# Five of six groups of an MLP's second product by Strassen's seven block products

## The chip, the core and the metric

The kernel runs on one core of a Trainium2 chip. The metric is the device time of one execution in microseconds (us), the median of several runs. The engines are named as in the profile: PE (TensorE, matrix products), DVE (VectorE), ACT (ScalarE), POOL (GpSimd) and SP (SyncE, which issues most DMAs). PE reads its operands from SBUF and writes to PSUM; DVE and ACT read both memories, POOL reads SBUF here.

## The reference

Linear attention with decay, then an MLP with a snake activation, on one set of 3072 tokens (4 batches of 768) with 512 features (8 heads of 64):

```python
for b in range(nb):                       # attention, block by block
    intra = einsum(qb, kb) * Dmask; intra = einsum(intra, vb)
    inter = einsum(qb * lam_pow, kv_state)
    out[:, :, sl] = intra + inter
    kv_state = lam_block * kv_state + einsum(kb_dec, vb)
x = out as (3072, 512)
h = x @ w_in                              # (3072, 512) @ (512, 2048)
s = sin(alpha * h)
g = h + s * s / (alpha + 1e-09)
return g @ w_out                          # (3072, 2048) @ (2048, 512)
```

Inputs and output are float32; the kernel multiplies in bf16 and accumulates in float32.

## The kernel before

The tokens are cut into six groups of 512 (`g` 0 to 5). A group has four attention units (`u` 0 to 23: one batch, four heads, 256 positions) and an MLP on its 512 tokens.

**A unit.** SP loads q, k and v (`ld`, 256 KB each). They are cast to bf16 (`cq`, `ck`, L717/L719), v is scaled (`sv`, L725 on POOL), q and k are transposed (`tq`, `tk` on PE with copies `e0`, `e1`; from unit 9 on by DMA). On PE follow scores (L759), products with the state (L869), the output (L882) and the update of the state (L793), from unit 8 on in one `step`. DVE masks the scores (`mm`, L767) and evicts the output into `xt` (`oe`, L901); ACT copies the state out (`kc`, L803); POOL decays and carries it (`d0`, `d1`, `n0`, `n1`: L818, L821, L859).

**The MLP.** A group has 16 f1 blocks, one for each 128 of the 2048 hidden columns: four matmuls of 128x128x512 into one PSUM bank (L916), a sine on ACT (`sn`, L923), a square on ACT or POOL (`sq`, L930/L932), and on DVE `g` = square times 1/alpha plus h into `gall` (L935), which releases the bank. The second product, f2, has for each of four token tiles (`m`) 16 matmuls of 128x128x512 (L952), in four blocks `f2_g_m_j`, added up in one bank; ACT copies it out (`ev`, L958) and SP stores it (`out`, L980). The last tile of group 5, `f2_5_3`, is made in two halves of 256 columns (`end0`, `end1`, `send0`, `send1`).

**Buffers.** f1 blocks, f2 tiles and some early transposes share four PSUM banks ("f"); of them f2 tiles may hold at most three at a time ("part"). `gall` has four buffers of a whole group.

**The order.** No loop gives the order. All steps are handed to a planner (`Plan`) as operations with a cost by engine, what they wait for, and a rank (`vt`); it plays them through and emits each engine's instructions in the order that it finds. `TUNE` shifts ranks and fixes engines, one entry per step. Each engine then works its instructions off in that order. On PE, f1 blocks of one group stand between steps of the units and f2 blocks of earlier groups; where f2 blocks are at hand they fill PE while the other engines work.

The costs that the planner uses for f1 and f2 blocks and the wait of f1 for a free `gall` buffer are these lines:

```python
mm = add(f"f1_{g}_{f}_{hb}", on("PE", .865 * x + (0.01 if hb is not None else 0)), ...)
op = add(f"f2_{g}_{m}_{j}", on("PE", .865), deps, vt, None, ...)
for g in range(NGB, NG):
    for f in range(NFC):
        f1_mm[g, f].after += [f2_last[g - NGB, m] for m in range(4)]
```

Of the kernel before, what the change touches and what calls it, by code (L numbers as in the profile page):

```python
# [167 lines left out]
def kernel(  # L168
# [11 lines left out]
    nc = tc.nc  # L180
# [15 lines left out]
        "lam": (0.0, 'ACT'), "iden": (0.0, 'POOL'), "lamb": (0.0, 'PE'), "tabc": (0.0, 'DVE'),  # L196
        "tab1": (1.2, 'POOL'), "tabm": (852.8, 'DVE'), "tabi": (-21.2, 'POOL'),
        "tabd": (-499.1, 'POOL'), "tab2": (-428.0, 'DVE'), "tab0": (-2.1, 'PE'),
        "tab4": (-818.2, 'DVE'), "tab3": (-962.3, 'ACT'), "alq": (0.0, 'ACT'),
# [1100 lines left out]
    for g in range(2, NG):  # L1300
        for f in range(NFC):
            make_f1(g, f, None)
# [45 lines left out]
```

## Time and profile before

| | |
|---|---|
| Time, median of 3 runs | 221.42 us (221.19 to 221.84) |
| Span of the profiled execution, first to last instruction | 218.2 us |
| The profiled execution's own time | not listed; the median lies 3.2 us above the span |
| Granted TensorE clock | 1.000 |
| PE busy | 211.9 us (97%), 2102 matmuls |
| DVE / ACT / POOL busy | 121.0 (55%) / 141.3 (65%) / 124.6 us (57%) |
| f1 matmuls (L916) | 388 |
| f2 matmuls (L952) | 400, of which 32 of 256 columns |
| HBM read / written | 27.27 / 6.29 MB |

Busy time of PE counts pipelined matmuls with modelled ends, so that what a matmul costs is better read from how many follow each other in a stretch than from the mean of one. On the other engines too an instruction may be recorded as starting a little before the last one's end. The chain of waits follows the end of the program back through whatever released each step. Idle time of an engine that is not the bottleneck costs nothing.

### The profile page before, as it was taken

The page shows a single profiled execution, that of the slowest core. Times are in us where ns is not written, and L with a number is a line of the kernel's source. Part 1 is how long each engine was busy: PE and PEld are TensorE (multiplying, and loading weights), DVE is VectorE, ACT ScalarE, POOL GpSimd, SP SyncE. Part 2 cuts the span into 40 slices and gives each one's busy share as a digit, 9 for nine tenths or more (in the row PEclk, how much of TensorE's full clock was granted, in tenths as well). Part 3 has the DMA queues.
Part 4 walks back from the last instruction along what each step waited for, and adds up shares of the span by engine and source line. Part 5 has one row for each costly group of instructions (what it writes and reads, how often), then busy time and mean ns, then how long its engine had stood idle before and what let it go on. Part 6 is the DMA issues. An engine that isn't in the chain of part 4 may idle for free.

```text
span 218.2 us, 5305 instructions
## 1 busy us (share of the span) xinstructions
PE 211.9 (97%) x2102; PEld 108.3 (50%) x2102; DVE 121.0 (55%) x176; ACT 141.3 (65%) x252; POOL 124.6 (57%) x209
## 2 busy tenths in 40 slices
PE   8999999999999999999999999999999999999994
PEld 3556644455544555545654545554444444444463
DVE  3457676457368974657794797975345451311100
ACT  3454699656499664878968787476778695634220
POOL 7959599768989899999898755611101100001000
PEclk9999999999999999999999999999999999999999
DMA  5999999898999999969999964020220221203164
GB/s 148 302 287 146 192 206 207 240 292 247 264 240 209 217 263 268 240 175 235 301 152 224 267 58 99 0 51 0 50 48 0 51 50 24 60 11 74 27 141 98
DMA packets 62139, 33.65 MB, mean 154 GB/s; under 512 B 17938, under 2 KB 59170, under 8 KB 62114
## 3 DMA queue, kind: packets, MB, share of 16 engines
q1 hardware_dynamic: 57776, 29.04, 59.5%
q0 software_dynamic: 4224, 4.19, 12.0%
q8 instruction: 16, 0.26, 0.5%
q10 hardware_dynamic: 114, 0.07, 0.1%
q14 instruction: 9, 0.07, 0.1%
HBM read 27.27 MB, written 6.29 MB: 154 GB/s over the span
## 4 chain that ended last, share of the span: by engine, by line
PE 90%; POOL 4%; issue 2%; ACT 1%; DVE 1%; POOLq 0%; ACTq 0%
PE hps L916 35%; PE ops L952 33%; PE bz L989 6%; PE sp L759 3%; PE okv L952 3%; PE okv L882 2%; PE pt L735 2%; PE okv L869 2%; PE okv L793 1%; POOL vb L725 1%; POOL kvs L859 1%; POOL qk L719 1%; PE kp L793 1%; DVE gall L935 1%; ACT s L923 1%
## 5 line engine op out<-in xcount | busy, mean ns | idle before, releaser
L935 DVE SCALAR_TENSOR_TENSOR gall<-s,r_sb,hps 128x512 bf16<-128x512 bf16 (+1 forms) x97 | 69.8, 740 | 63.7 <-ACT s L930 47.8
L916 PE MATMUL hps<-xt,w_in_sb 128*128 128x512 bf16 (+1 forms) x388 | 91.9, 377 | 1.4 <-DVE gall L935 0.8
L952 PE MATMUL ops<-w_out_sb,gall 128*128 128x512 bf16 (+1 forms) x368 | 83.1, 370 | 0.0
L923 ACT ACTIVATE s<-hps,alpha_sb 128x512 bf16<-128x512 f32 (+1 forms) x97 | 65.4, 679 | 25.9 <-PE hps L916 24.7
L952 PEld LDWEIGHTS <-gall 128*128 128x128 bf16 x400 | 38.5, 98 | 41.7
L916 PEld LDWEIGHTS <-w_in_sb 128*128 128x128 bf16 x388 | 36.5, 98 | 43.2 <-issue 2.6
L932 POOL TENSOR_TENSOR s<-s 128x512 bf16<-128x512 bf16 x21 | 21.9, 1041 | 51.9 <-ACT s L923 51.9
L930 ACT ACTIVATE s<-s 128x512 bf16<-128x512 bf16 (+1 forms) x76 | 46.6, 623 | 1.7
L767 DVE TENSOR_TENSOR sm<-sp,mask 128x1024 bf16<-128x1024 f32 x24 | 29.3, 1220 | 4.6 <-PE sp L759 4.5
L725 POOL TENSOR_TENSOR vb<-st_v,R 128x512 bf16<-128x512 f32 x24 | 25.0, 1045 | 2.5 <-DMA st_v<-in_v_dram 2.5
L958 ACT COPY ob<-ops 128x512 f32<-128x512 f32 x21 | 12.3, 584 | 20.2 <-PE ops L952 20.2
L821 POOL TENSOR_TENSOR kvbd<-kvx,LBD 128x256 bf16<-128x256 f32 x32 | 19.7, 614 | 2.5
L818 POOL TENSOR_TENSOR kvx<-kva,kvs 128x128 f32<-128x128 f32 x32 | 14.6, 456 | 7.8 <-ACT kva L803 7.7
L901 DVE TENSOR_TENSOR xt<-okv,ET 128x512 bf16<-128x512 f32 x24 | 16.5, 686 | 3.1 <-PE okv L882 2.8
L989 PE MATMUL bz<-const-bfloat16-1.0 128*128 128x256 bf16 (+1 forms) x69 | 16.4, 311 | 1.5 <-PEq L1332 0.8
L719 POOL CAST qk<-st_q 128x512 bf16<-128x512 f32 x19 | 11.5, 612 | 2.5 <-PE okv L793 2.5
L719 POOL CAST qk<-st_k 128x512 bf16<-128x512 f32 x17 | 10.4, 613 | 0.8 <-DMA st_k<-in_k_dram 0.8
L759 PE MATMUL sp<-qt 64*64 64x128 bf16 x384 | 10.0, 221 | 0.0
L882 PE MATMUL okv<-sm,vb 64*64 64x128 bf16 x384 | 9.7, 218 | 0.0
L859 POOL TENSOR_TENSOR kvs<-kvx,ET 128x128 f32<-128x128 f32 x24 | 9.4, 403 | 0.0
L803 ACT COPY kva<-okv 128x256 f32<-128x256 f32 (+1 forms) x16 | 5.0, 314 | 6.6 <-PE okv L793 6.4
L742 ACT COPY qt<-pt 128x512 bf16<-128x512 bf16 x9 | 5.2, 590 | 6.2 <-PE pt L735 6.2
(63 smaller groups left out, 110.7 us busy)
## 6 DMA issues: line engine op xcount, KB each, us to landing
st_q<-in_q_dram SPq DMA_DIRECT2D x24, 256.0 KB, 5.1
st_k<-in_k_dram SPq DMA_DIRECT2D x24, 256.0 KB, 5.3
st_v<-in_v_dram SPq DMA_DIRECT2D x24, 256.0 KB, 5.0
out_dram<-ob SPq DMA_DIRECT2D x46, 128.0 KB, 2.5
w_out_sb<-in_moe_w_out_dram POOLq DMA_DIRECT2D x4, 512.0 KB, 11.9
w_in_sb<-in_moe_w_in_dram POOLq DMA_DIRECT2D x2, 512.0 KB, 6.4
w_in_sb<-in_moe_w_in_dram POOLq DMA_DIRECT2D x1, 768.0 KB, 9.6
w_in_sb<-in_moe_w_in_dram POOLq DMA_DIRECT2D x1, 256.0 KB, 6.4
```

What stands on the lines that cost most here:

```text
L719: ENGINE[op.eng].tensor_copy(out=o, in_=i)
L725: ENGINE[op.eng].tensor_tensor(out=T[u, "vb"][:], in0=T[u, "v"][:].rearrange("p h two e -> p two h e"), in1=R[:, :, hs].unsqueeze(3).to_br ...
L759: nc.tensor.matmul(out=T[u, "sp"][half[c], hd, par, hp, :], lhsT=QT[half[hd], 1, par, hp, half[c]], rhs=QT[half[hd], 0, :, hp, half[c]], s ...
L767: V.tensor_tensor(out=T[u, "sm"][:].rearrange("p hd par hp i -> p (hd par) hp i"), in0=T[u, "sp"][:].rearrange("p hd par hp i -> p (hd par ...
L821: G.tensor_tensor(out=bd[:], in0=X.unsqueeze(2).to_broadcast([P, 2, 2, D]), in1=LBD[:, hs, :].unsqueeze(3).to_broadcast([P, 2, 2, D]), op= ...
L916: op.ins = nc.tensor.matmul(out=op.tile[:, cols], lhsT=w_in_sb[:, c, f * P:(f + 1) * P], rhs=xt[g][:, c].rearrange("p b c i -> p (b c i)") ...
L923: A.activation(out=op.tile[:, cols], in_=mm.tile[:, cols], func=ACTF.Sin, scale=alpha_sb[:, f:f + 1])
L930: A.activation(out=op.tile[:, cols], in_=s1, func=ACTF.Square)
L932: ENGINE[op.eng].tensor_tensor(out=op.tile[:, cols], in0=s1, in1=s1, op=ALU.mult)
L935: V.scalar_tensor_tensor(out=gall[g][:, f, cols], in0=sq.tile[:, cols], scalar=r_sb[:, f:f + 1], in1=mm.tile[:, cols], op0=ALU.mult, op1=A ...
L952: op.ins = nc.tensor.matmul(out=first.tile[:, cols], lhsT=gall[g][:, f, m * P:(m + 1) * P], rhs=w_out_sb[:, f, cols], start=(f == 0), stop ...
L989: nc.tensor.matmul(out=bz[:, :w], lhsT=nc.const_aps.tensor(1.0, [P, P], BF16), rhs=nc.const_aps.tensor(1.0, [P, w], BF16), start=True, sto ...
```

## The change

For groups 1 to 5 the second product is cut into 2x2 blocks: 256 tokens by the even or odd hidden tiles, and even or odd hidden tiles by 256 output columns. Instead of eight block products, seven are made, with sums of blocks as operands, and the four output blocks are put together from the seven. Group 0 keeps the plain product.

- `wsum` (`wb_k_a`): five sums of blocks of w_out, in halves, 10 instructions of 128x1024 once, on DVE or POOL.
- `gsum` (`ca_g_k_h`): five sums of blocks of `gall` for each group, in halves `h` by hidden tiles 0 to 7 and 8 to 15, 10 instructions of 128x1024 per group on DVE or POOL. Seven buffers hold them, four of which lie in parts of `w_out_sb` that are no longer needed.
- `prod` (`p1` to `p7`): each product is 2 token tiles x 8 pairs of hidden tiles = 16 matmuls of 128x128x256, in two blocks of eight. Products 3 and 5, 2 and 4, 1 and 7 are added up in the same bank, with reads in between (`m3`, `e`, `x`).
- In float32: m3 = P3, e = m3 - P2, c12 = P3 + P5, c21 = P2 + P4, u = c21 - c12, w = u + e, x = e + P1, c11 = w + P1 + P7, c22 = x + P6.
- `m3`, `c12`, `c21` on ACT and `e`, `u`, `w`, `x`, `c11`, `c22` on DVE (`u`, `w` on DVE or POOL) put the output together in float32. The store is two DMAs of 256 KB for each half of the tokens; for the last group `p6` is made and stored in two token tiles.
- `gall` is now five buffers of half a group (`NGH`); f1 waits for the readers of the half that it overwrites.
- Set-up tensors share space with work buffers, `kvbd` and `kvx` get rotating buffers, and all `TUNE` entries are new. The cost rules of the planner are unchanged.

The diff, cut to its core:

```diff
-    NOB = 3
-    NGB = 4
+    STR = (1, 2, 3, 4, 5)
+    NAC = 7
+    NPT = 4
+    NOA = 2
+    NGH = 5
+    NBD = (5, 10)
...
+    wb = consts.tile([P, 5, NPR, DH], BF16, name="wb")
...
-        if g not in gall:
-            gall[g] = gbp.tile([P, NFC, 512], BF16, name="gall")
+        if (g, f // 8) not in gall:
+            gall[g, f // 8] = gbp.tile([P, 8, 512], BF16, name="gall", tag=f"gall{(2 * g + f // 8) % NGH}")
...
+    GSUM = {0: ((0, 0), (1, 1), ALU.add), 1: ((1, 0), (1, 1), ALU.add),
+            2: ((0, 0), (0, 1), ALU.add), 3: ((1, 0), (0, 0), ALU.subtract),
+            4: ((0, 1), (1, 1), ALU.subtract)}
+    PROD = {"1": (0, 0), "2": (1, (0, 0)), "3": ((0, 0), 1), "4": ((1, 1), 2),
+            "5": (2, (1, 1)), "6": (3, 3), "7": (4, 4)}
+    def wsum(op, k, a, n):
+        (p0, c0), (p1, c1), alu = WSUM[k]
+        ENGINE[op.eng].tensor_tensor(out=wb[:, k, a:a + n, :], in0=pairs(w_out_sb, p0, colh[c0], a, n),
+                                     in1=pairs(w_out_sb, p1, colh[c1], a, n), op=alu)
+    def gsum(op, g, k, a, n):
+        i = op.bank["ac"][0]
+        if i < 4:
+            comb[g, k, a // 4] = pairs(w_out_sb, i % 2, colh[1 - i % 2], i // 2 * 4, 4)
+        else:
+            comb[g, k, a // 4] = combp.tile([P, 4, 2 * C], BF16, name="ac", tag=f"ac{i}")[:]
+        (t0, p0), (t1, p1), alu = GSUM[k]
+        gh = gall[g, a // 4]
+        ENGINE[op.eng].tensor_tensor(out=comb[g, k, a // 4], in0=pairs(gh, p0, colh[t0], 0, n),
+                                     in1=pairs(gh, p1, colh[t1], 0, n), op=alu)
+    def prod(op, g, x, to, a, n, begin, ms=(0, 1)):
+        ga, wa = PROD[x]
+        for m in ms:
+            for i in range(a, a + n):
+                ...
+                op.ins = nc.tensor.matmul(out=to[:, m, :], lhsT=lhs, rhs=rhs, ...)
...
+            for n, k in enumerate((1, 2, 0, 4, 3)):
+                more = [ca[k, 0]] if h else (wb_all + f2_end[0] if g == STR[0] else ca_last)
+                if n > 1:
+                    more = more + [ca[1, h], ca[2, h]]
+                ca[k, h] = add(f"ca_{g}_{k}_{h}", [("DVE", .71), ("POOL", 2.1)], deps + more, ...)
...
+        p3 = product("3", bp, (), take=fp)
+        m3 = part("m3", on("ACT", .6), [p3], ...)
+        p2 = product("2", bq, (), take=fp, after=[pe["3", 0]])
+        e = part("e", on("DVE", .7), [m3, p2], ...)
+        p5 = product("5", bp, (), begin=False, after=[m3])
+        p4 = product("4", bq, (), begin=False, after=[e])
+        c12 = part("c12", on("ACT", .6), [p5], ...)
+        c21 = part("c21", on("ACT", .6), [p4], ...)
+        u = part("u", [("POOL", 1.05), ("DVE", .7)], [c12, c21], ...)
+        w = part("w", [("POOL", 1.05), ("DVE", .7)], [u, e], ...)
+        p1 = product("1", br, (), take=fp, after=[pe["2", 0]])
+        x = part("x", on("DVE", .7), [p1, e], ...)
+            p7 = product("7", br, (), begin=False, after=[x])
+            c11 = part("c11", on("DVE", .7), [p7, w, c12], ...)
+            p6 = product("6", bt, (), take=fp, after=[pe["1", 0]])
+            c22 = part("c22", on("DVE", .7), [p6, x, c21], ...)
...
+            add(f"out_{g}_0", on("SP", 1.0), [c11, c12], vt + 28, ...)
+            add(f"out_{g}_1", on("SP", 1.0), [c21], vt + 17, ...)
+                add(f"send{m}", on("SP", 1.0), [c22], vt + 28 + m, ...)
...
-            f1_mm[g, f].after += [f2_last[g - NGB, m] for m in range(4)]
+            s = 2 * g + f // 8 - NGH
+            if s >= 0:
+                f1_mm[g, f].after += read[divmod(s, 2)]
```

In the order that comes out, 35 of the 50 sums of `gall` stand on DVE and 15 on POOL, 8 of the 10 sums of w_out on DVE and 2 on POOL, 5 of the 10 `u` and `w` on either; four `qt` copies move from DVE to ACT, and all 16 f1 blocks of group 0 stand ahead of the first f2 block. In the changed program a product is at L1112, a sum of `gall` at L1099, `sv` at L839, casts at L833.

More of the change, by code (lines that the diff above doesn't have):

```diff
@@ L195 @@
     TUNE = {
[L196 to L199, printed above, removed]
[285 rows of a table removed]
+        "lam": (439.7, None), "iden": (-4413.2, None), "lamb": (-2596.0, None),
+        "tabc": (-1807.6, None), "tab1": (2107.4, None), "tabm": (-2161.9, None),
+        "tabi": (-4543.5, None), "tabd": (-4933.7, None), "tab2": (-2633.1, None),
+        "tab0": (-3592.8, None), "tab4": (-3002.1, None), "tab3": (-2939.9, None),
+        "alq": (-1078.2, None), "alpha": (-3139.3, None), "alphav": (-2326.7, None),
[389 rows of a table added]
     }
@@ L568 @@
                  "vb": list(range(NVB)), "sm": list(range(NSM)), "s1": list(range(NML)),
-                 "s2": list(range(NML)), "ob": list(range(NOB)), "part": list(range(NPART))})
+                 "s2": list(range(NML)), "part": list(range(NPART)),
+                 "ac": list(range(NAC)), "pt": list(range(NPT)), "oa": list(range(NOA))})
     add = plan.add
@@ L581, in sync_dep @@
             mybir.DependencyClass.Sync, mybir.DependencyReason.DATA))
-    ones = consts.tile([P, P], FP32, name="ones")
+    ones = work.tile([P, P], FP32, name="ones", tag="qt3")
     warm = consts.tile([1, 1], FP32, name="warm")
@@ L601 @@
                allow_small_or_imprecise_dtypes=True)
-    it = consts.tile([P, 2, D], FP32, name="it")
+    it = work.tile([P, 2, D], FP32, name="it", tag="sm1")
     G.iota(out=it[:], pattern=[[1, 2], [2, D]], base=0, channel_multiplier=0,
@@ L608 @@
     make_identity(nc, idf[:])
-    id2 = consts.tile([P, D], FP32, name="id2")
+    id2 = work.tile([P, D], FP32, name="id2", tag="vb4")
     for c in range(2):
@@ L621 @@
     E2 = consts.tile([P, HP, 2], FP32, name="E2")
-    ED = consts.tile([P, HP * 2, D], FP32, name="ED")
+    ED = work.tile([P, HP * 2, D], FP32, name="ED", tag="sm2")
     ET = consts.tile([P, HP, 2, D], FP32, name="ET")
@@ L680 @@
     w_out_sb = consts.tile([P, NFC, DM], BF16, name="w_out_sb")
+    NPR = NFC // 2
+    DH = DM // 2
+    wb = consts.tile([P, 5, NPR, DH], BF16, name="wb")
     def load_w_in(op, a, w):
@@ L833, in decay_first @@
         hs = slice(2 * hh, 2 * hh + 2)
[L834 removed]
+        bd = kvp.tile([P, 2, 2, D], BF16, name="kvbd0", bufs=NBD[0])
         V.tensor_tensor(out=bd[:],
@@ L934, in f1g @@
     def f1g(op, mm, sq, g, f, cols):
-        V.scalar_tensor_tensor(out=gall[g][:, f, cols], in0=sq.tile[:, cols],
+        V.scalar_tensor_tensor(out=gall[g, f // 8][:, f % 8, cols], in0=sq.tile[:, cols],
                                scalar=r_sb[:, f:f + 1], in1=mm.tile[:, cols],
@@ L952, in f2mm @@
             op.ins = nc.tensor.matmul(
-                out=first.tile[:, cols], lhsT=gall[g][:, f, m * P:(m + 1) * P],
+                out=first.tile[:, cols], lhsT=gall[g, f // 8][:, f % 8, m * P:(m + 1) * P],
                 rhs=w_out_sb[:, f, cols], start=(f == 0), stop=(f == NFC - 1))
-    def f2ev(op, first):
-        op.tile = slot(op, outp, "ob", [P, DM], FP32)
-        A.copy(out=op.tile[:], in_=first.tile[:])
-    def f2end(op, first, cols):
-        op.tile = slot(op, outp, "ob", [P, DM], FP32)
-        o = op.tile[:, cols]
-        if op.eng == "ACT":
-            A.copy(out=o, in_=first.tile[:, cols])
-        else:
-            V.tensor_copy(out=o, in_=first.tile[:, cols])
@@ L968, in f2send, with pairs @@
-    def f2send(op, ev, g, m, cols, queues):
-        _, tp, b, _, _ = where(4 * g + 2 * (m // 2))
-        r0 = b * S + tp * W + (m % 2) * C
-        rows = out[r0:r0 + C, cols].rearrange("(p two) d -> two p d", two=2)
-        for par in range(2):
-            queues[par].dma_start(out=rows[par], in_=ev.tile[par * D:(par + 1) * D, cols])
+    def pairs(t, par, cols, a, n):
+        return t[:, 2 * a + par:2 * (a + n) - 1 + par:2, cols]
+    GSUM = {0: ((0, 0), (1, 1), ALU.add), 1: ((1, 0), (1, 1), ALU.add),
+            2: ((0, 0), (0, 1), ALU.add), 3: ((1, 0), (0, 0), ALU.subtract),
+            4: ((0, 1), (1, 1), ALU.subtract)}
@@ new lines, in prod @@
+    def prod(op, g, x, to, a, n, begin, ms=(0, 1)):
+        ga, wa = PROD[x]
+        for m in ms:
+            for i in range(a, a + n):
+                if isinstance(ga, tuple):
+                    lhs = gall[g, i // 4][:, 2 * (i % 4) + ga[1],
+                                          ga[0] * 2 * C + m * C:ga[0] * 2 * C + (m + 1) * C]
+                else:
+                    lhs = comb[g, ga, i // 4][:, i % 4, m * C:(m + 1) * C]
+                rhs = w_out_sb[:, 2 * i + wa[0], colh[wa[1]]] if isinstance(wa, tuple) else wb[:, wa, i, :]
+                op.ins = nc.tensor.matmul(out=to[:, m, :], lhsT=lhs, rhs=rhs,
+                                          start=(begin and i == 0 and m == ms[0]), stop=(i == NPR - 1),
+                                          skip_group_check=True)
@@ L975, in f2st @@
+    def f2ev(op, first):
+        op.tile = slot(op, outp, "oa", [P, 2, DM], FP32)[:, 0]
+        A.copy(out=op.tile, in_=first.tile[:])
     def f2st(op, ev, g, m):
@@ L979, in f2st @@
         for par in range(2):
-            SY.dma_start(out=rows[par], in_=ev.tile[par * D:(par + 1) * D, :])
+            SY.dma_start(out=rows[par], in_=ev.tile[par * D:(par + 1) * D])
     PEL = 0.22
@@ L1189 @@
     lent_by = {}
-    def make_f2_end(g, m):
-        vt = 32 * (g + 1) + 8 * m
-        prev = None
-        for k, cols in enumerate((slice(0, DM // 2), slice(DM // 2, DM))):
-            first = None
-            for j in range(4):
-                deps = [f1_done[g, f][None] for f in range(4 * j, 4 * j + 4)]
-                op = add(f"f2_{g}_{m}_{j}{'ab'[k]}", on("PE", .44), deps + [prev], vt + 4 * k + j, None,
-                         take=("f", "part") if j == 0 else (), lag=PEL if j == 3 else -0.05, mode="n")
-                first = first or op
-                op.emit = lambda op, j=j, first=first, cols=cols: f2mm(op, first, g, m, j, cols)
-                prev = op
-            if k == 0:
-                ev = add("end0", on("ACT", .4), [prev], vt + 4 * k, lambda op, first=first, cols=cols:
-                         f2end(op, first, cols), take=("ob",), give=((first, "f"), (first, "part")))
-                add("send0", on("SP", 1.0), [ev], vt, lambda op, ev=ev, cols=cols:
-                    f2send(op, ev, g, m, cols, (SY, SY)))
-            else:
-                ev = add("end1", on("DVE", .35), [prev], vt + 4, lambda op, first=first, cols=cols:
-                         f2end(op, first, cols), take=("ob",))
-                add("send1", on("SP", 1.0), [ev], vt, lambda op, ev=ev, cols=cols:
-                    f2send(op, ev, g, m, cols, (SY, A)))
     def make_f2(g, m):
@@ L1246, in make_f2, with make_wsums @@
         ev = add(f"ev_{g}_{m}", on("ACT", .57), [blocks[3]], vt - 6, lambda op: f2ev(op, blocks[0]),
-                 take=("ob",), give=owe)
+                 take=("oa",), give=owe)
         st = add(f"out_{g}_{m}", on("SP", 1.0), [ev], vt - 6, lambda op: f2st(op, ev, g, m),
-                 give=((ev, "ob"),), dma=(.65, .08))
+                 give=((ev, "oa"),), dma=(.65, .08))
         f2_last[g, m] = blocks[3]
+    wb_ops = {}
+    def make_wsums():
+        for a in range(0, NPR, 4):
+            for k in (1, 0, 2, 3, 4):
+                wb_ops[k, a] = add(f"wb_{k}_{a}", [("DVE", .71), ("POOL", 2.1)],
+                                   [wo[f] for f in range(2 * a, 2 * a + 8)], 30 + a + k,
+                                   lambda op, k=k, a=a: wsum(op, k, a, 4))
@@ L1252, with f2store @@
+    def f2store(tile, g, half_, cols, queues, m=None):
+        _, tp, b, _, _ = where(4 * g + 2 * half_)
+        r0 = b * S + tp * W
+        ms = range(2) if m is None else (m,)
+        n = len(ms)
+        r0 += C * ms[0]
+        rows = out[r0:r0 + C * n, cols].rearrange("(m p two) d -> two p m d", m=n, two=2)
+        for par in range(2):
+            queues[par].dma_start(out=rows[par], in_=tile[par * D:(par + 1) * D, ms[0]:ms[0] + n, cols])
     for u in range(8):
@@ L1302 @@
             make_f1(g, f, None)
+    make_wsums()
+    wb_all += wb_ops.values()
+    read = {}
     for g in range(NG):
+        if g in STR:
+            make_f2_blocks(g)
+            continue
         for m in range(4):
-            (make_f2_end if (g, m) == (NG - 1, 3) else make_f2)(g, m)
-    for g in range(NGB, NG):
+            make_f2(g, m)
+        f2_end[g] = [f2_last[g, m] for m in range(4)]
+        read[g, 0] = read[g, 1] = f2_end[g]
+    for g in range(NG):
         for f in range(NFC):
-            f1_mm[g, f].after += [f2_last[g - NGB, m] for m in range(4)]
+            s = 2 * g + f // 8 - NGH
+            if s >= 0:
+                f1_mm[g, f].after += read[divmod(s, 2)]
     for u in range(4 * NXT, NU):
```

127 lines of the change are left out of this document (123 added, 4 removed), and 674 rows, old and new, of the table TUNE.

## The prediction

> **What bounds the kernel now.** I read the page first, then the chain of waits, then busy time by stage, the groups with shapes kept apart, and the order in time at both ends.
>
> ```profile
> PE 211.9 (97%) x2102; PEld 108.3 (50%) x2102; DVE 121.0 (55%) x176; ACT 141.3 (65%) x252; POOL 124.6 (57%) x209
> PE   8999999999999999999999999999999999999994
> POOL 7959599768989899999898755611101100001000
> ```
> PE is full in all slices but the first and the last; POOL comes next, full to about 140 us and idle behind. The stages say it sharper (columns: window, length, busy PE, PEld, DVE, ACT, POOL with instruction counts, granted clock, DMA):
>
> ```profile
> 57.60:67.10 9.50, 8.46 (x45) 3.72 (x47) 5.06 (x8) 8.49 (x14) 8.83 (x12) 1.00 1.05 253
> 67.10:143.20 76.10, 76.10 (x990) 40.50 (x990) 56.73 (x74) 56.71 (x102) 63.18 (x107) 1.00 0.94 188
> 143.20:200.30 57.10, 57.10 (x322) 26.46 (x321) 23.56 (x32) 37.51 (x61) 6.27 (x7) 1.00 0.17 38
> ```
> From 67.1 us on PE never stands, so there a matmul taken away is time taken away, as long as PE's inputs still come in time. In that stage POOL is 83% busy, DVE and ACT 75% each. The end of the chain prices the matmuls:
>
> ```profile
> 200.27 13.85 PE ops L952 x80
> 214.13 0.78 PE bz L989 x7
> ```
> The 80 are 48 of 512 columns and 32 of 256 (`f2_5_3` in two halves), 64 full ones in all: 13.85/64 = 0.216 us for 512, 0.108 for 256.
>
> **The matmuls.** A plain group has 64 matmuls of 512 columns, 64 x 0.216 = 13.82 us. Seven products of 16 matmuls of 256 columns are 112 x 0.108 = 12.10. That is 1.73 less in each of five groups: **-8.6 us**. The order of the changed program shows 560 such matmuls and 64 of 512, so the saving is really in it. Each 256-column matmul has its own weight load; the 32 above had too and ran at 0.108, and transposes (L735), four with four loads, follow each other in 0.22, 0.055 each: the load does not set the pace.
>
> **The end.** Before, what is left when PE has done its last product is a 0.42 us copy and 64 KB pieces:
>
> ```profile
> 212.46 0.59 ACT L958 COPY ob<-ops 128x512 f32<-128x512 f32 x1 [0.49 <-PE ops L952]
> 213.19 1.19 SPq L980 DMA_DIRECT2D out_dram<-ob  x2
> 214.22 0.42 DVE L966 COPY ob<-ops 128x256 f32<-128x256 f32 x1 [11.78 <-PE ops L952]
> 214.67 0.47 SPq L973 DMA_DIRECT2D out_dram<-ob  x1
> ```
> ```profile
> out_dram<-ob SPq DMA_DIRECT2D x46, 128.0 KB, 2.5
> out_dram<-ob SPq DMA_DIRECT2D x3, 64.0 KB, 2.0
> ```
> Span minus end of PE's products is 218.2 - 214.1 = 4.1. After, `c11_5` needs `p7_5_1`, which stands one block (0.86) ahead of PE's end; with 0.2 of signal and 0.69 it is done about as PE ends, and only then SP issues `out_5_0`, two DMAs of 256 KB, 0.55 each, with the last 64 KB piece on SP queued behind them. From 2.0 for 64 KB and 2.5 for 128 KB, 256 KB land in 3.5, two together in 4 to 5 (inputs of 256 KB under load take 5.1). Second issue at +0.65 behind PE's end, landing some 4.3 later, and 1.3 that the span has today behind its last landing (214.67 + 2.2 for the piece on ACT's queue = 216.9): 6.2, so **+2.2 us** (1 to 3).
>
> **The additions.** Costs by row:
>
> ```profile
> L935 DVE SCALAR_TENSOR_TENSOR gall<-s,r_sb,hps 128x512 bf16<-128x512 bf16 x95 | 68.9, 745 | 62.6 <-ACT s L930 46.7 <-POOL s L932 15.7
> L767 DVE TENSOR_TENSOR sm<-sp,mask 128x1024 bf16<-128x1024 f32 x24 | 29.3, 1220 | 4.6 <-PE sp L759 4.5
> L932 POOL TENSOR_TENSOR s<-s 128x512 bf16<-128x512 bf16 x21 | 21.9, 1041 | 51.9 <-ACT s L923 51.9
> L901 DVE TENSOR_TENSOR xt<-okv,ET 128x512 bf16<-128x512 f32 x24 | 16.5, 686 | 3.1 <-PE okv L882 2.8
> L719 DVE CAST qk<-st_k 128x512 bf16<-128x512 f32 x1 | 0.4, 363 | 0.0
> ```
> ACT: three copies of 0.585 a group in place of four; four more of the `qt` copies (0.59), three more squares (0.63), three fewer casts (0.62): its sum stays within 1 us, no cost.
>
> DVE and POOL get 50 sums of g halves (`ca`, 35 on DVE, 15 on POOL), 10 sums of w_out (8 and 2), and per group four fp32 combinations with a PSUM input (0.69 like L901) and two with both inputs in SBUF (`u`, `w`). On POOL a sum of 1024 elements is twice L932, 2.08. On DVE no row shows one: L767, as many elements at one per cycle, says 1.22; twice L719, at two per cycle, 0.73, or 0.65 without its fixed part twice. All operands are bf16 in SBUF, nearest to L719: I take 0.65. The Trainium skill, "VectorE: DVE Perf Modes", section on the perf-mode tier table, gives bf16 tensor_tensor in SBUF two elements per cycle, 0.69 by its 1224 ns for 2048 elements less the fixed part; no row here shows it, and the sum would be the same within 2 us.
>
> Now the stage from `step8` to `step23`. In the new order PE has 57 f1 blocks, 32 product blocks and 15 steps in it: 89 x 0.864 + 15 x 1.02 = 92.1 us (a step takes 1.02 between its neighbours, e.g. 70.13 to 71.15). DVE has 57 g, 16 masks, 15 `oe`, 22 `ca`, 2 `u`/`w`, 8 other combinations. Back to back an instruction starts 0.08 before the last one's recorded end (two g in 1.41), so 57 x 0.66 + 16 x 1.13 + 15 x 0.60 + 24 x 0.65 + 8 x 0.61 = 85.2, 93% of the stage where it was 75%. POOL has 76.1 by durations, 72.7 by starts (0.04 less each). Both fit, barely: alone this gives PE short waits. Three of the four f banks can be held by products, so a late g reaches PE within one or two f1 blocks. Before, with DVE at 53% but ACT at 89% in 57.6 to 67.1, PE lost 1.0 us. I take **+1.0** (0 to 4), the start of the kernel included, where all f1 blocks of group 0 now precede the first f2 block and ACT sets the pace as before.
>
> **What two SBUF inputs cost.** At the start of the trace one DVE instruction has both inputs in SBUF:
>
> ```profile
> 1.70 0.69 DVE L614 TENSOR_TENSOR mask<-it,jt 128x512 bf16<-128x512 f32 x1 [0.30 <-POOL it L603]
> 1.89 0.65 POOL masks.py:199 TENSOR_SCALAR_AFFINE_SELECT iden<-iden 128x128 bf16<-128x128 bf16 x1
> 2.67 0.19 POOL masks.py:199 TENSOR_SCALAR_AFFINE_SELECT idf<-idf 16x16 f32<-16x16 f32 x1
> 3.02 0.23 POOL masks.py:199 TENSOR_SCALAR_AFFINE_SELECT id<-id 64x64 f32<-64x64 f32 x1
> ```
> POOL's select of 16 columns takes 0.19, of 64 columns 0.235: 0.175 fixed and 0.001 per column, so 128 columns should take 0.30. Under the mask it took 0.65 and ended 0.15 after it: as if held until the mask was done at 2.39. Later DVE instructions of any weight read at most one tensor in SBUF (the other is in PSUM), and POOL's rows keep their length beside them. The new `ca`, `wb`, `u`, `w` have both inputs in SBUF, and POOL works beside them. If each excludes the other, a DVE sum waits for the POOL instruction under way, about half of one, 0.42 (POOL's mix of 0.40 to 2.08), and holds up POOL for 0.61. In the stage: DVE 85.2 + 24 x 0.42 = 95.3, POOL 72.7 + 24 x 0.61 = 87.3, against 92.1. At least 3.2 over, at most the 10.1; behind a waiting `ca` stand the g that free PE's banks. I take 4.0. From `step23` to the end 16 such DVE sums meet eight POOL sums of 2.08: `p5_4` waits for `ca_4_2` on DVE, which becomes ready with POOL's `ca_4_1` (one to two times about 1), and group 5 alternates `ca_5_0`, `ca_5_2` on DVE with four on POOL. I take 3.0 (0 to 5). Together **+7.0** (0 to 15).
>
> The Trainium skill has this as a rule: "SBUF — State Buffer", section "Who interferes with whom", says that a DVE instruction with two SBUF inputs contends with a GpSimd instruction that reads SBUF, and that the later one blocks until the earlier is done. The mask row agrees with it for a POOL instruction that comes second; none shows DVE second.
>
> **The sum.** The profiled span is 218.2; its own whole time is not listed, and 3.2 lie between the span and the median of 221.4, which I keep. Span 218.2 - 8.6 + 2.2 + 1.0 + 7.0 = 219.8, time **223.0 us**. Chance 0.55, its own range 217 to 230: I am surer of the saving than of the wait.
>
> **Rivals.** (1) The sums of DVE and POOL pass each other, or wait only where DVE has slack. For it: both engines fit without the wait, the evidence is a single row of a short instruction, and buffers (four f1 banks, four `qk`, five `vb`) let POOL run some 15 us ahead of PE (`sv23` at 126, its step at 143). Then the 7.0 goes: 216.0 (213.5 to 219), faster. It decides if DVE's `ca` keep a length below 0.75 while POOL is busy. Chance 0.35.
> (2) The DVE sums are slow in themselves or lose every turn. At 1.22 each, 24 x 0.57 = 13.7 more in a stage that is already 3.2 over gives 16.9 in place of 4.0: 236. A DVE sum that waits for two POOL instructions rather than half of one, about 1.4, comes out as far up. Against: L719 is twice as fast as one per cycle, and a waiting instruction should get its turn. Chance 0.10.
> That the products aren't replaced is excluded by the order.
>
> **The numbers.** What this kernel's measurement can tell is about 0.3%, 0.7 us. Faster by more than that: nearly all of rival 1 and an eighth of the forecast, 0.34 + 0.06 = 0.40. Within: 0.06. Slower: the rest, 0.54. Of both signs the likeliest is 223; the range goes from rival 1's lower part to where rival 2 begins, 214.5 to 230.
>
> **What would show it.** PE's products L1112 at 0.108 each, 60.5 us for five groups, and no gap but behind `ca`: right in the first step. `ca` rows (L1099) on DVE at 0.7 to 1.5, spread wide, with POOL rows of a kind (L839, L833) longer than 1.045 and 0.612: right in the wait; all at one length: rival 1; all at 1.2: rival 2. PE idle released by DVE `gall` or `ca` of 5 to 10 us between 60 and 200 us. At the end a span that goes on 6 us after PE's last product. I am wrong if DVE's work in the stage runs below 90% while PE waits, or if PE's gaps sit before 60 us.

## The result, and the profile after

The changed kernel takes 234.06 us (median of 4 runs, 231.80 to 235.88); the kernel before, run beside it, 221.63. The ratio is 1.0528, 95% interval 1.0474 to 1.0581; it leaves out the run of 235.88 us, which fell into a slower state of the core, and so lies below 234.06/221.63. The profiled execution took 234.59 with a span of 232.8: 14.6 more than before. The forecast was 223.0, in a range of 214.5 to 230: the sign is right, the size is not.

The page (busy time by engine, then the slices of PE, DVE, POOL and the granted clock):

```profile
PE 210.0 (90%) x2326; PEld 131.8 (57%) x2326; DVE 184.4 (79%) x240; ACT 140.4 (60%) x252; POOL 179.4 (77%) x230
...
PE   8998999887999999889898969968999998699792
...
DVE  3365666998679999799899967999795689979950
ACT  3464798543399976756585755573747765583110
POOL 7969759997999999999999999894673239028820
PEclk9999999999999999999999999997999999999998
```
PE has holes now, from the eighth slice (41 us) to the end. DVE went from 121 to 184 us and POOL from 125 to 179. With the same instructions at their free lengths they would stand at 159 and 164 (the page of the first experiment, `one_input`); the other 25 and 15 us are waits.

By stage (window, length, busy PE, PEld, DVE, ACT, POOL, clock, DMA): from 19 us up to the mask of unit 8, to that of unit 23, to PE's last product.

```profile
19.00:64.60 45.60, 41.94 (x477) 20.81 (x477) 34.69 (x45) 27.66 (x56) 39.46 (x57) 1.00 1.02 215
64.60:169.90 105.30, 96.96 (x1224) 62.20 (x1213) 95.30 (x120) 73.33 (x129) 96.98 (x126) 0.98 0.73 155
169.90:227.00 57.10, 52.53 (x405) 37.86 (x404) 46.02 (x55) 30.09 (x48) 27.92 (x17) 1.00 0.17 43
```
In the middle stage DVE and POOL are busy some 90 and 92%, ACT 70%, and yet PE stands for 8.3 us. Two engines that wait for each other inside their instructions would look like that, since the profile counts such a wait as busy. But the shares alone do not show it: in `one_input`, the first experiment, both have the same shares of that stage, and PE stands for only 1.3 us (85.4 and 87.3 of 94.4 us; the row stands further down). The rows show it. First the page's groups, then the order in time around the w_out sums and around PE's widest gap:

```profile
L839 POOL TENSOR_TENSOR vb<-st_v,R 128x512 bf16<-128x512 f32 x24 | 26.3, 1099 | 0.0
L1099 DVE TENSOR_TENSOR w_out_sb<-gall 128x1024 bf16<-128x1024 bf16 x20 | 25.1, 1261 | 0.1
...
L1099 POOL TENSOR_TENSOR ac<-gall 128x1024 bf16<-128x1024 bf16 x8 | 19.1, 2397 | 6.4 <-DVE gall L1049 4.8
...
L1099 DVE TENSOR_TENSOR ac<-gall 128x1024 bf16<-128x1024 bf16 x15 | 19.7, 1322 | 1.3 <-PE ops L1112 1.3
...
L1099 POOL TENSOR_TENSOR w_out_sb<-gall 128x1024 bf16<-128x1024 bf16 x7 | 16.6, 2379 | 0.0
```
```profile
41.03 0.68 DVE L1088 TENSOR_TENSOR wb<-w_out_sb 128x1024 bf16<-128x1024 bf16 x1
...
42.29 2.32 DVE L1088 TENSOR_TENSOR wb<-w_out_sb 128x1024 bf16<-128x1024 bf16 x1
...
45.85 7.39 DVE L1088 TENSOR_TENSOR wb<-w_out_sb 128x1024 bf16<-128x1024 bf16 x6
```
```profile
41.94 2.12 POOL L1088 TENSOR_TENSOR wb<-w_out_sb 128x1024 bf16<-128x1024 bf16 x1
44.01 1.07 POOL L833 CAST qk<-st_q 128x512 bf16<-128x512 f32 x1
45.05 2.11 POOL L1088 TENSOR_TENSOR wb<-w_out_sb 128x1024 bf16<-128x1024 bf16 x1
47.12 1.49 POOL L839 TENSOR_TENSOR vb<-st_v,R 128x512 bf16<-128x512 f32 x1
48.56 1.07 POOL L833 CAST qk<-st_k 128x512 bf16<-128x512 f32 x1
49.59 1.48 POOL L839 TENSOR_TENSOR vb<-st_v,R 128x512 bf16<-128x512 f32 x1
51.02 1.07 POOL L833 CAST qk<-st_q 128x512 bf16<-128x512 f32 x1
```
The sum at 41.03 began as a POOL instruction ended (41.08) and took 0.68, its free length; it held the POOL instruction that began at 41.04, which took 0.94 for 0.40. The next began at 42.29, in POOL's 41.94 to 44.06, and lasted until 44.61, which is 0.55 after POOL's end. The others do the same: of DVE's 43 sums of `gall` and w_out 35 begin under a POOL instruction, and each of the 35 ends 0.54 to 0.56 us after it. The six at 45.85 take turns with POOL's instructions until POOL has none left at 52.1, 1.23 each, and the four POOL instructions that begin under them are 0.45 longer than free (a cast 1.07 for 0.61, `sv` 1.49 for 1.045), as the cast at 44.01 is under the sum before. Around 156 us:

```profile
149.56 2.12 POOL L1099 TENSOR_TENSOR ac<-gall 128x1024 bf16<-128x1024 bf16 x1 [0.86 <-DVE gall L1049]
...
150.65 1.58 DVE L1099 TENSOR_TENSOR w_out_sb<-gall 128x1024 bf16<-128x1024 bf16 x1
...
151.64 2.58 POOL L1099 TENSOR_TENSOR w_out_sb<-gall 128x1024 bf16<-128x1024 bf16 x1
...
152.81 1.95 DVE L1099 TENSOR_TENSOR w_out_sb<-gall 128x1024 bf16<-128x1024 bf16 x1
...
154.18 2.56 POOL L1099 TENSOR_TENSOR ac<-gall 128x1024 bf16<-128x1024 bf16 x1
...
154.69 2.60 DVE L1099 TENSOR_TENSOR ac<-gall 128x1024 bf16<-128x1024 bf16 x1
...
157.22 1.39 DVE L1049 SCALAR_TENSOR_TENSOR gall<-s,r_sb,hps 128x512 bf16<-128x512 bf16 x2
...
158.00 1.49 PE L1030 MATMUL hps<-xt,w_in_sb 128*128 128x512 bf16 x5 [2.64 <-DVE gall L1049]
```
Three DVE sums wait behind three POOL sums, 6.1 us in place of 2.0; the `g` that frees PE's bank stands behind the last of them, and PE stands for 2.64 us. The Trainium skill's rule that the prediction cited ("SBUF — State Buffer", section "Who interferes with whom") holds here in both directions, the one with DVE second included, which no row of before showed. This exclusion is called the lock from here on.

The end is as forecast: PE's last product ends at 226.9, the span at 232.8, 5.9 later (4.1 before).

The chain of waits tells the same by shares of the span; before, PE had 90% of it, POOL 4% and DVE 1%.

```profile
PE 43%; POOL 25%; DVE 21%; ACT 5%; issue 4%; POOLq 0%; DVEq 0%; ACTq 0%
```

### The profile page after: what moved, and what is told of

The parts are those of the page before. It is cut to its first block, busy times and chain, and to the rows that moved or that the text cites. A ratio compares the mean times of both kernels' runs of the same rounds, so it can differ in the third digit from the quotient of the medians.

```text
span 232.8 us, 5816 instructions
## 1 busy us (share of the span) xinstructions
PE 210.0 (90%) x2326; PEld 131.8 (57%) x2326; DVE 184.4 (79%) x240; ACT 140.4 (60%) x252; POOL 179.4 (77%) x230
## 4 chain that ended last, share of the span: by engine, by line
PE 43%; POOL 25%; DVE 21%; ACT 5%; issue 4%; POOLq 0%; DVEq 0%; ACTq 0%
PE ops L1112 17%; PE hps L1030 14%; PE bz L1134 6%; DVE gall L1049 6%; DVE w_out_sb L1099 6%; POOL vb L839 5%; POOL qk L833 5%; POOL kvbd L935 4%; DVE ac L1099 4%; DVE wb L1088 3%; POOL s L1046 3%; POOL kvx L932 3%; POOL kvs L973 3%; ACT s L1037 2%; ACT s L1044 2%
## 5 line engine op out<-in xcount | busy, mean ns | idle before, releaser
L1046 POOL TENSOR_TENSOR s<-s 128x512 bf16<-128x512 bf16 x18 | 18.6, 1040 | 16.9 <-ACT s L1037 16.7
L839 POOL TENSOR_TENSOR vb<-st_v,R 128x512 bf16<-128x512 f32 x24 | 26.3, 1099 | 0.0
L1099 DVE TENSOR_TENSOR w_out_sb<-gall 128x1024 bf16<-128x1024 bf16 x20 | 25.1, 1261 | 0.1
L1112 PEld LDWEIGHTS <-w_out_sb 128*128 128x128 bf16 x216 | 20.9, 98 | 5.9 <-issue 1.3
L1099 POOL TENSOR_TENSOR ac<-gall 128x1024 bf16<-128x1024 bf16 x8 | 19.1, 2397 | 6.4 <-DVE gall L1049 4.8
L1112 PEld LDWEIGHTS <-ac 128*128 128x128 bf16 x184 | 18.4, 100 | 6.6 <-DVE ac L1099 1.3
L1099 DVE TENSOR_TENSOR ac<-gall 128x1024 bf16<-128x1024 bf16 x15 | 19.7, 1322 | 1.3 <-PE ops L1112 1.3
L1112 PE MATMUL ops<-wb,gall 128*128 128x256 bf16 x160 | 19.3, 273 | 1.5 <-DVE pt L1448 1.5
L1112 PEld LDWEIGHTS <-gall 128*128 128x128 bf16 x160 | 15.6, 98 | 5.3 <-issue 1.7
L1112 PE MATMUL ops<-wb,w_out_sb 128*128 128x256 bf16 x144 | 18.2, 273 | 0.0
L1099 POOL TENSOR_TENSOR w_out_sb<-gall 128x1024 bf16<-128x1024 bf16 x7 | 16.6, 2379 | 0.0
```

Of the source, the lines that this page charges most:

```text
L839: ENGINE[op.eng].tensor_tensor(out=T[u, "vb"][:], in0=T[u, "v"][:].rearrange("p h two e -> p two h e"), in1=R[:, :, hs].unsqueeze(3).to_br ...
L1046: ENGINE[op.eng].tensor_tensor(out=op.tile[:, cols], in0=s1, in1=s1, op=ALU.mult)
L1099: ENGINE[op.eng].tensor_tensor(out=comb[g, k, a // 4], in0=pairs(gh, p0, colh[t0], 0, n), in1=pairs(gh, p1, colh[t1], 0, n), op=alu)
L1112: op.ins = nc.tensor.matmul(out=to[:, m, :], lhsT=lhs, rhs=rhs, start=(begin and i == 0 and m == ms[0]), stop=(i == NPR - 1), skip_group_c ...
```

## Experiments

To tell stages apart I use two kinds of times of each trace: the starts of the masks (`sm`, one for each unit) of units 0, 8 and 23, and the end of PE's last product. The kernels of this table have one order of instructions, so the differences between these lengths are waits and the edits' own durations.

| | unit 0 to 8 | 8 to 23 | 23 to PE's end | time, us |
|---|---|---|---|---|
| changed kernel | 55.7 | 105.3 | 57.0 | 234.06 |
| `one_input` | 53.0 | 94.4 | 52.7 | 216.05 |
| `one_input_long` | 54.3 | 97.7 | 53.1 | 222.10 |
| `pool_short` | 56.3 | 99.5 | 52.5 | 223.41 |
| `one_input_w` | 53.2 | 106.7 | 57.0 | 232.18 |
| `one_input_g123` | 55.9 | 94.4 | 57.0 | 223.49 |
| `two_halves` | 56.0 | 106.9 | 62.9 | 242.13 |
| `pool_quarters` | 56.0 | 105.5 | 52.8 | 230.03 |

The profiled execution of `pool_short` took 224.97, 1.6 over its median, so its lengths are too long by as much in sum; the others lie within 1.5 of theirs.

**`one_input`: the same order, without the second SBUF input.**

```diff
+        if op.eng == "DVE":          # gsum; wsum, u and w on DVE likewise
+            V.tensor_reduce(out=dst.bitcast(FP32), in_=pairs(gh, p1, colh[t1], 0, n).bitcast(FP32).unsqueeze(3),
+                            axis=mybir.AxisListType.X, op=ALU.max)
+            return
         ENGINE[op.eng].tensor_tensor(out=dst, in0=pairs(gh, p0, ...), in1=pairs(gh, p1, ...), op=alu)
```

In this and the next cuts of code `dst` stands for `comb[g, k, a // 4]`, and the arguments are shortened.

> The changed kernel with the same order of instructions on every engine, the same buffers and products; but each sum on DVE (35 of gall, 8 of w_out, 5 u or w) becomes one instruction with one SBUF input, which reads the first or second block alone as 512 words of fp32 (0.6 us by the nearest rows, where the free sum took 0.68) and writes the whole tile, so that the sum itself is left out. Theory A (a DVE sum with both inputs in SBUF and a POOL instruction exclude each other, and that is the stall): without the second input the sums stand at about 0.6 us whatever POOL does, POOL's rows go back to 1.045 (sv) and 0.612 (casts), and the time falls to 216 (214 to 220), faster than before. Rival B (the new order, PSUM banks held by products, or the half-group buffers make PE wait): all of that is kept, so 229 or more. Rival C (DVE has simply too much to do): its number of instructions and nearly its time by free durations are kept, so 227 or more.

Measured: 216.05 us (214.70 to 217.18), ratio to before 0.9745 (0.9700 to 0.9791). The new instructions, by the groups of its trace (DVE's sums of gall, then `sv` and POOL's sums):

```profile
L1090 DVE TENSOR_REDUCE w_out_sb<-gall 128x512 f32<-128x512 f32 x20 | 13.5, 680 | 4.0 <-PE ops L1123 3.9
L1090 DVE TENSOR_REDUCE ac<-gall 128x512 f32<-128x512 f32 x15 | 10.0, 678 | 0.6 <-PE ops L1123 0.6
```
```profile
L839 POOL TENSOR_TENSOR vb<-st_v,R 128x512 bf16<-128x512 f32 x24 | 25.0, 1046 | 0.2 <-PE okv L996 0.2
...
L1110 POOL TENSOR_TENSOR ac<-gall 128x1024 bf16<-128x1024 bf16 x8 | 17.0, 2125 | 4.8 <-DVE gall L1049 4.8
```
0.68 us is to the hundredth what the free sum takes, so DVE has the same work, the order, buffers and banks are the same, and only the second input is gone: 18.0 us. Rivals B and C are out. The chain of waits is PE's again:

```profile
PE 80%; DVE 7%; ACT 5%; POOL 3%; issue 2%; POOLq 0%; ACTq 0%
```

**`one_input_w`: only the eight w_out sums.** Edit: the same, in `wsum` alone.

> As the changed kernel, but only the eight w_out sums on DVE have one SBUF input (the sum left out); the gall sums are untouched. In the changed kernel PE fell 3.7 us further behind before step8, with these eight sums (10.4 us on DVE, 1.35 each) at 41 to 53 us. Theory A: those 3.7 come back and nothing else: 230.3 (229 to 232). Rival B or C: less than 1 us, 233 to 234.5.

Measured: 232.18 us (230.19 to 232.59), 1.9 less. The first stage gained 2.5 of the 3.7 expected, and the next lost 1.4 of it again.

**`one_input_long`: the lock gone, the length kept.** Edit: as `one_input`, with `in_` and `out` left in bf16, 1024 elements.

> As the kernel with one SBUF input in all DVE sums, but these read 1024 elements of bf16 one at a time: about 1.15 us each, nearly as long as the sums in the changed kernel with their waits (1.28 mean), while POOL is not held. It tells which side of the lock costs the time. If it is DVE's lengthened sums (DVE late with g): 227 to 232. If it is POOL held up by DVE: 216 to 220. Rival C (DVE's load): as the former.

Measured: 222.10 us (220.84 to 223.33), ratio 1.0022 (0.9997 to 1.0046); the DVE instructions took 1.21, POOL's rows were free. It lies between the two cases: 43 longer DVE instructions cost 6 of the 18 us. What the other 12 come from this run does not part: besides the holds of POOL it leaves out that the waits are uneven, up to 1.9 us and in bunches, where here every instruction is 0.53 longer.

**`pool_short`: POOL's sums short.**

```diff
+        if op.eng == "POOL":
+            nc.gpsimd.tensor_copy(out=dst.bitcast(FP32), in_=pairs(gh, p1, colh[t1], 0, n).bitcast(FP32))
+            return
```

> As the changed kernel, but POOL's 15 gall sums become one-input copies of 512 words (about 0.6 in place of 2.12 to 2.57 us; the sums left out); DVE's sums keep two inputs. Theory A: DVE's longest waits (2.3 to 2.6 us, behind POOL's sums) go, and the 2.6 us gap of PE behind gall near 156 us and the end's wait for e_5 with them; the other waits stay: 229 (226 to 232). Rival C: DVE unchanged, 233 to 235. If POOL's own sums were the bound: 222 or less.

Measured: 223.41 us (221.00 to 225.58), 10.7 less than the changed kernel and twice what I gave it. With two SBUF inputs still, DVE's sums fell from 1.26 and 1.32 to:

```profile
L1103 DVE TENSOR_TENSOR w_out_sb<-gall 128x1024 bf16<-128x1024 bf16 x20 | 16.6, 837 | 1.3 <-PE ops L1116 1.2
...
L1103 DVE TENSOR_TENSOR ac<-gall 128x1024 bf16<-128x1024 bf16 x15 | 12.1, 814 | 0.5 <-PE ops L1116 0.5
```
In the last stage the whole loss of 4.3 goes with POOL's sums (52.5, against 52.7 without any lock), in the middle over half. But the edit shortens two things: POOL's longest instructions, and POOL's work, by 25 us (its sums from 35.7 to 10.9). The next kernel parts them.

**`pool_quarters`: POOL's sums cut, its work kept.**

```diff
+        for i in range(n) if op.eng == "POOL" else (slice(0, n),):
+            ENGINE[op.eng].tensor_tensor(out=dst[:, i], in0=pairs(gh, p0, ...)[:, i], in1=pairs(gh, p1, ...)[:, i], op=alu)
```

> The changed kernel, with each of POOL's 15 sums of gall cut into four instructions of 256 elements (about 0.61 each by the rows of kvbd, 2.3 in all by starts: POOL gets 3 to 4 us more work, not less; the same result). It parts what the kernel with short POOL sums left together: the length of POOL's instructions and its amount of work. Theory A (turns: DVE waits for the instruction that POOL has under way, and now that is a quarter): DVE's sums fall to about 0.85 as with short POOL sums, and of the 10.7 us most come back: 226 (224 to 229). If the 10.7 were POOL's load: no gain, 233 or more.

Measured: 230.03 us (229.09 to 232.90), 4.0 less than the changed kernel, where I had 8.

```profile
L1100 DVE TENSOR_TENSOR w_out_sb<-gall 128x1024 bf16<-128x1024 bf16 x20 | 19.7, 993 | 0.2 <-PE ops L1113 0.2
```
```profile
L1100 POOL TENSOR_TENSOR ac<-gall 128x256 bf16<-128x256 bf16 x32 | 24.4, 791 | 2.5 <-PE ops L1113 2.5
L1100 POOL TENSOR_TENSOR w_out_sb<-gall 128x256 bf16<-128x256 bf16 x28 | 23.2, 858 | 0.0
```
DVE's sums fall to 0.99, POOL's grow from 35.7 (19.1 + 16.6) to 47.6 us. The table parts the two causes by stage: at the end, where POOL has little else to do, the shorter turn alone gives all of the 4.2 back; in the middle nothing is left of it (105.5). The starts of the masks show why. Up to unit 20 the stage grows by 3.0 us (84.2 for 81.2): in the changed kernel POOL has no pause over 0.2 us from 54 to 148.7 us, and its work has grown here. From unit 20 to 23 it shrinks by 2.7 (21.3 for 24.0): there lies the bunch of long turns at 150 to 158 us. So where POOL is full its load counts, lengthened by every hold, and where its long sums meet DVE's the turn counts. Both of my cases were half right.

**`one_input_g123`: where the price is paid.** Edit: as `one_input` in `gsum`, for `g < 4` only; w_out, `u`, `w` untouched.

> The changed kernel, with one SBUF input (the sum left out) only in DVE's sums of gall for groups 1 to 3; those of groups 4 and 5, of w_out, and u and w are as in the changed kernel. By the masks' starts, the kernel with one input everywhere gained 2.7 us on the changed one before step8 (with the w_out sums), 10.9 from there to step23 and 4.3 after. Theory A: the 10.9 come back, less what groups 4 and 5 now lose in a stage that they begin earlier: 224.5 (222 to 227). If the wait is carried by the late groups (POOL's four sums of group 5, the end): 229 or more.

Measured: 223.49 us (222.02 to 227.21), ratio 1.0095 (1.0056 to 1.0134). By the table the stages are separable: 94.4 in the middle as with no lock at all, 57.0 at the end and 55.9 at the start as with all of it.

**`two_halves`: twice the turns, the same bytes.**

```diff
+        for c in (slice(0, C), slice(C, 2 * C)) if op.eng == "DVE" else (slice(0, 2 * C),):
+            ENGINE[op.eng].tensor_tensor(out=dst[:, :, c], in0=pairs(gh, p0, ...)[:, :, c], in1=pairs(gh, p1, ...)[:, :, c], op=alu)
```

> The changed kernel, with each of DVE's 35 sums of gall cut into two instructions of 512 elements (two SBUF inputs as before; the same elements, the same result). Free, the two take some 0.1 us more than one. Theory A in its form by turns (the lock goes from instruction to instruction; a DVE sum that finds POOL at work waits until POOL's instruction ends, whatever its own length): twice as many turns, so each sum that meets POOL waits for one more POOL instruction of about 0.6 to 1.0 us, and DVE, late already, passes that on: 246 (240 to 254). Rival D (the two share the ports in proportion to what they move, without turns): the same bytes, 234 to 237.

Measured: 242.13 us (241.07 to 242.72), 8.1 slower than the changed kernel. A half sum takes as long as 0.85, where a whole one free takes 0.68:

```profile
L1100 DVE TENSOR_TENSOR w_out_sb<-gall 128x512 bf16<-128x512 bf16 x40 | 32.3, 850 | 0.1
```
The shortest half takes 0.41, so the two halves of a sum wait 0.88 together, where a whole sum waits 0.60 for the same bytes. The wait is for turns, not for bytes; rival D is out. Most of the loss came in the last stage (5.9), where POOL's long sums are.

**`replan_all`: the same work in an order that knows the lock.** Its `TUNE` is new; the rule added to the planner is:

```diff
+                if e == "DVE" and op.name.split("_")[0] in ("ca", "wb", "u", "w"):
+                    if free["POOL"] > t:
+                        c += free["POOL"] - t
+                    lock = t + c - LOCKB          # 0.3
+                if e == "POOL" and t < lock and not op.dma:
+                    c += lock - t
```

> The same work as the changed kernel (Strassen in groups 1 to 5, all sums with two inputs), with another order: the planner is given the lock as a rule (a DVE instruction with two SBUF inputs that begins while POOL works lasts until POOL's instruction ends and 0.71 us more; a POOL instruction that would begin meanwhile waits until 0.3 us before the sum's end) and ranks and engines are searched anew under it; the planner's cost of a product block is 0.866 in place of 0.885, as measured. Theory A: with the rule played over the changed kernel's own order, PE's last product ends at 228.6 (226.9 in the trace, 206.8 without the rule), over the new order at 217.5; with the 7.2 us that lay between PE's end and the time there, 224.7 (222 to 228): the order gives back half of what the lock took, the rest stays since the sums and POOL still meet. If the stall comes from elsewhere: no gain, 232 or more.

Measured: 229.33 us (228.18 to 229.90), ratio 1.0358 (1.0312 to 1.0403). PE's last product ended at 221.3, 3.8 later than the rule had it. The order gives back 4.7 of the 18.0, half of what I expected of it; the gain confirms the direction, and a plan made to the last tenth by a rule is not kept by the chip.

**`replan_345`: Strassen in three groups.** With the planner's rule and a new `TUNE`:

```diff
-    STR = (1, 2, 3, 4, 5)
+    STR = (3, 4, 5)
...
+            add(f"out_{g}_2", on("SP", 1.0), [c12], vt + 16, lambda op: f2store(st["o1"], g, 0, colh[1], (SY, SY)), ...)
-            add(f"out_{g}_0", on("SP", 1.0), [c11, c12], vt + 28, lambda op: f2store(st["o1"], g, 0, slice(0, DM), (SY, SY)), ...)
+            add(f"out_{g}_0", on("SP", 1.0), [c11], vt + 28, lambda op: f2store(st["o1"], g, 0, colh[0], (SY, A)), ...)
```

> Strassen in groups 3, 4 and 5 alone (groups 1 and 2 plain), planned with the lock as a rule and searched likewise; the store of group 5's first half is cut so that its finished columns leave early and only 128 KB halves follow PE's end, on two queues. 30 sums of gall in place of 50, most of them after POOL's dense stage. Theory A: PE's last product at 210.8 by the rule, and 7.2 less some 0.8 for the shorter store to the time: 217.3, or 219 with the 1.9 us by which the same planner put the kernel before too early: 218.5 (216.5 to 221.5), faster than both kernels. If the lock isn't what counts, the saving of three groups (5.2 us) less the end's 1 us would give 217.

Measured: 223.12 us (221.05 to 226.05), ratio to before 1.0061 (1.0027 to 1.0094), 4.6 over what I expected and no gain. The expectation's plan broke early: in the profiled execution, 1.9 over the median, unit 0's mask starts at 8.9 for 7.2 planned, unit 9's at 71.0 for 65.1, unit 20's at 143.5 for 136.3, so that all of some 7 arise ahead of the first `ca` (149.2), 5.9 of them by unit 9; at 59.5 to 62.4 POOL stood 2.88 us for a load. What failed is the planner's picture of the start, the loads at least among it.

**`replan_345_quarters`.** Edit: the same with POOL's sums (of gall and w_out) cut as in `pool_quarters`.

> Strassen in groups 3 to 5 with the searched order, POOL's sums (of gall and of w_out) cut into quarters in the same way. Theory A: DVE's 16 sums, 1.06 to 1.14 on average there, fall to about 0.85, some 4 us less of DVE's time, of which a part is on PE's path: 221.5 (219.5 to 223.5), about level with the kernel before. If POOL's load sets that kernel's pace: 224 or more.

Measured: 222.92 us (220.98 to 225.58), ratio 1.0050 (1.0024 to 1.0076): the same as without the cut. DVE's sums went from 1.06 and 1.14 to 0.94 and 1.10, and the time did not change. So three groups of Strassen about break even (half a percent slower), and no kernel here computes the reference faster than the one before.

## Why the prediction was wrong, point by point

**The matmuls, -8.6: right.** The products run at the forecast pace:

```profile
209.48 8.75 PE ops L1112 x80
218.83 2.01 DVE ac L1099
221.49 5.40 PE ops L1112 x48
```
80 in 8.75 us and 48 in 5.40 (the second with the pipeline's end in it) are 0.109 and 0.112 each; 0.108 was forecast. The gap between the two rows, released by `ac`, is the kind of gap that the prediction named.

**The end, +2.2: right.** 5.9 us from PE's last product to the end of the span instead of 4.1: +1.8, in `one_input` the same (208.2 to 214.1).

**The additions, +1.0: right.** A free sum takes 0.68 (0.65 taken). In `one_input` the stage from unit 8 to 23 is 94.4 long, where the prediction put 92.1 of PE and 1.0 of short waits. By the times, 221.34 - 8.6 + 1.8 + x = 216.05 gives x = 1.5. With the lock away the sum came out to 0.1 us: rival 1 had 216.0. That it is so close is luck, as -0.4 in the end and +0.5 in the additions cancel, and one reading under it was wrong: POOL's load in the stage (below).

**What two SBUF inputs cost, +7.0 (0 to 15): the mechanism right, the size wrong.** This is the step that failed: 18.0 us were measured (234.06 - 216.05; 17.3 by the two ratios). It failed in three places.

First, at the end. The prediction has that "a DVE sum waits for the POOL instruction under way, about half of one, 0.42": measured are 1.28 - 0.68 = 0.60 on average, but the mean isn't the price. Behind POOL's own sums, whose 2.12 us I had listed and averaged away, DVE's sums last 1.6 to 2.6 us, and they come in bunches, when both engines' sums become ready together (150.65 to 157.22 above is such a bunch, still in the middle stage). From `step23` on that is the whole of 4.3 (3.0 forecast): cutting or shortening POOL's sums alone removes it.

Second, in the middle, 10.9 where I had 4.0. I compared each engine's sum with PE's and took the larger excess, DVE's 95.3 against 92.1. But POOL's load in that sum, 72.7 us, was too low. `one_input`, without any hold, shows it in the same stage (window, length, busy PE, PEld, DVE, ACT, POOL, clock, DMA):

```profile
61.10:155.49 94.39, 93.12 (x1205) 61.58 (x1213) 85.37 (x119) 73.23 (x129) 87.30 (x125) 1.00 0.83 176
```
DVE's 85.4 is the prediction's 85.2, POOL's 87.3 is 14.6 more than it had. With 24 holds of 0.61, as I took them, POOL would have come to 101.9, nearly 10 over PE's 92.1; with the measured 0.45 it comes to 98.1, and DVE with the measured 0.60 a sum to 99.6. Neither alone gives 105.3; the rest is that the waits chain. POOL, full and held again and again, is late with `kvbd`, which PE's step needs:

```profile
140.15 0.34 PE L983 MATMUL okv<-qt,kvbd 128*128 128x128 bf16 x3 [2.64 <-POOL kvbd L935]
```
PE is then late with f1, so is `g`, and behind it stands the next sum. Of PE's longer waits in the stage 3.9 us are for `g` and 3.4 for `kvbd`. By the masks, 6.5 of the 10.9 arise up to unit 20, while POOL never pauses for more than 0.2 us, and 4.4 from there to unit 23, where the bunch stands. `one_input_long` shows that DVE's length alone is 3.3 of the 10.9; `pool_short` takes 5.8 away, with less work on POOL and shorter turns together. POOL, 83% busy before, was the engine to add up with its holds inside the order, not beside it. That its load set the pace up to unit 20 is read from the trace and from `pool_quarters`; no run here lightens POOL alone.

Third, for the start the lock was priced at nothing; the prediction only has that "all f1 blocks of group 0 now precede the first f2 block and ACT sets the pace as before". The eight w_out sums stand on DVE in front of `kvbd` and the masks of units 5 to 7, and cost 2.5 to 2.7 us before unit 8. The last of its signs of being wrong, "if PE's gaps sit before 60 us", names it. By stage the lock cost 2.7, 10.9 and 4.3, where I had 0, 4.0 and 3.0.

A smaller share that no step had: behind the second 2.64 us gap (155.4 to 158.0) PE's clock fell (window, length, busy times, clock):

```profile
158.00:161.40 3.40, 3.40 (x12) 1.58 (x12) 3.40 (x5) 1.28 (x2) 1.33 (x2) 0.63 0.00 0
```
Eight matmuls of 512 columns took 2.77 there instead of 1.90 (at 141.11). The changed kernel's profiled run (clock 0.988 over the span) took 234.59, one at 1.000 took 231.80: with the clock up to 2.3 of the 18.0 may go (234.06 - 231.80). The Trainium skill, "TensorE: Matmul & The Clock Gate", section "Why this matters for your kernels", asks for no idle gap over about 3 us between bursts; here one of 2.64 stood right before the drop. But the gap of the same length at 137.5 us brought none, so that the lock's holes cause the drops is not shown.

**The rivals.** Rival 1 had the right test (sums under 0.75 while POOL works), and its answer was no. Rival 2 came nearest in time (236), but by luck: the sums are not slow in themselves (0.68 free, not 1.22), and its second form, a wait of 1.4 a sum, is far from the 0.60 measured. What holds of it is that the waits are longer than half an instruction. I gave it 0.10 on the ground that "a waiting instruction should get its turn"; it does get it, and behind a POOL sum the turn costs up to 1.9 us.

## What to carry to other kernels

Before work is moved to DVE, list which of its new instructions read two tensors from SBUF and which POOL instructions can be under way then. Count the work of both engines in each stage anew, from the order as it will be. Price each meeting at what is left of that POOL instruction, not at a mean, keep long POOL instructions away from sums that stand ahead of an eviction that PE waits for, and where POOL is already full add its holds to its load. And read a high busy share of DVE and POOL with care: compare one row's mean with its shortest instance, for a wait on the other engine is counted as work.

## What the runs showed of the hardware

- The lock goes by turns, instruction by instruction: DVE's sums and POOL's instructions alternate as long as both have work (45.85 to 52.09 us above). A sum that begins under a POOL instruction ends 0.55 us after it. Two half sums wait 0.88 us, a whole one 0.60, and with its extra instructions the cut costs 8 us.
- A DVE sum of 0.68 us holds POOL for 0.45 in 29 of 35 cases (0.33 to 0.54 in the others), not for its whole length.
- A TENSOR_REDUCE over an axis of one, on bf16 pairs read as fp32, takes 0.68 for 512 words as well, and neither waits for POOL nor holds it; the Trainium skill says of tensor_reduce that it never contends on this chip ("SBUF — State Buffer", section "Who interferes with whom"), and the rows agree: `sv` 1.046 beside it, 1.099 beside sums.
